# A fused attention, FFN and routed-expert kernel: the router's logits from plain float32 products on four column tiles at once

## The chip, the cores and the metric

The kernel runs on one core of a Trainium2 chip. Its time is the device time of one execution in microseconds (us), as a median over runs. The profile is of one execution.

## The reference

Three stages follow each other on 2304 tokens (4 batches of 576):

```
attn:  8 heads of 64, block-causal softmax attention             -> x [2304, 512]
moe:   h = sigmoid(x @ w_gate) * (x @ w_val)   (d_ff 1536);  x2 = h @ w_out
moe2:  logits = x2 @ w_gate2   (8 experts)
       every token goes to one expert in the order of falling logits, at most 288 tokens an expert
       out[token] = relu(x2 @ w1[e]) @ w2[e]
```

All of it is float32. The assignment of tokens depends on the order of all logits, so these are wanted to float32's full precision.

## The kernel before, in words

TensorE multiplies float32 in two ways here. A *plain* float32 product is one call that appears as two weight loads and two matmuls in the trace. A call on operands stored as F32R (float32r) appears as one weight load and one matmul; for these the kernel splits each operand into a high part (a copy rounded to F32R) and a low part (the difference), and adds the three products high x high, high x low, low x high. The profile's shapes show F32R operands of matmuls as f32 too.

*First half* (`first_half`). For each batch b of 576 tokens, `Ffn.batch` runs 12 tiles f of 128 columns of d_ff. For each tile, two halves hf of 288 tokens; for each half, gate and value: 4 x 3 matmuls of 288 columns into one PSUM bank (L457). ScalarE takes tanh of the gate (L469), VectorE makes h (L470), and SP stores h to memory in the next tile (`store`, L319). While a tile runs, the next tile's weights are split (`split`: ScalarE copies, GpSimd subtracts) and the one after is loaded. `batch` is a generator: each `yield` is a step, and `first_half` uses the steps to interleave other work by count or by cost: attention of the next batch (batches 0 to 2), and every fourth step of batch 3 one advance of `rl` and one of `wo`. `rl` is the chain `relogits(0)`, `relogits(1)`, `f2.first()`; `wo` loads and splits w_out. What is left of `rl` when batch 3 ends is drained there.

*Logits.* As logits are linear in h, the kernel multiplies h by `wog`, the product of w_out and the router's weights, made in batch 1 by `router_weights` (12 tiles of 128 x 8). In batches 2 and 3 (`inline`) h is split while it is made: ScalarE copies it to hh (L472), VectorE subtracts to hl a little later (L474, the list `late`). For every two tiles f, `logits` multiplies hh and hl of both by 128 columns of `wog`, which hold the high and the low part of the weights in columns 0 to 7 and 32 to 39 and zeros elsewhere: 4 matmuls of 288 columns for each half (L410), and VectorE copies or adds the result to `lt` (L414, L416). The last group of batch 3 is in `ffn.close` and is run among the first matmuls of the second FFN, as `CLOSE` counts them. For batches 0 and 1, whose h were made before `wog` existed, `relogits` loads h again, two tiles at a time (L502), splits it (L511 on ScalarE, L512 on VectorE) and multiplies. At the end of each batch `rows` turns `lt` into one row for each token by matmuls with `sel` (L425, L427), which also adds the two partial sums in rows 0 to 7 and 32 to 39.

*Second FFN and router.* `Ffn2.run` multiplies h by w_out, token tile by token tile (L687, 36 products of 512 columns each). `first` loads the first two tiles of h (L647) and splits the first (L660 on ScalarE, L664 on GpSimd), ahead of `run`. The router (`Router.run`) searches the assignment on VectorE with small matmuls and is interleaved with the second FFN's steps by the counts in FILL, FIRST and TAIL; what is left of the second FFN is drained after it. Then the experts follow.

Each engine carries out its instructions in the order in which they were written, and SP issues the DMAs in order too: a load whose buffer isn't free holds up all behind it. All matmuls write to one pool of 8 PSUM banks (`psA`).

Of the kernel before, what the change touches and what calls it, by code (L numbers as in the profile page):

```python
# [8 lines left out]
F32 = mybir.dt.float32  # L9
F32R = mybir.dt.float32r  # L10
BF16 = mybir.dt.bfloat16
I32 = mybir.dt.int32
AF = mybir.ActivationFunctionType
# [3 lines left out]
P = 128  # L17
# [3 lines left out]
def f32(ap):  # L21
    return ap.bitcast(F32)
# [274 lines left out]
class Ffn:  # L297
# [27 lines left out]
    def load(self, b, f, j):  # L325
        k, nc = self.k, self.k.nc
        if b >= k.nb:
            return
        if b == 0:
            x = self.r64.tile([P, 512, 2], I32, name="w64")  # L330
            nc.sync.dma_start(x.rearrange("p (k f) t -> p k (f t)", k=4),
                              (k.w_gate, k.w_val)[j].bitcast(I32)[:, f * 256:(f + 1) * 256]
                              .rearrange("(k p) f -> p k f", p=P))
        else:
            x = self.wf.tile([P, 512], F32, name=f"wf{j}")
            nc.sync.dma_start(x, k.wgv_d[f, j])
        self.raws[b, f, j] = x
# [62 lines left out]
                yield  # L400

    def logits(self, lt, g, hs):
        k, nc = self.k, self.k.nc
        for hf in range(2):
            t = k.psA.tile([P, 512], F32, name="A")
            n = 0
            for f in range(2):
                w = k.wog[:, (2 * g + f) * 64:(2 * g + f) * 64 + P]
                for x in hs[f]:
                    nc.tensor.matmul(t[:, 0:288], w, x[:, hf * 288:(hf + 1) * 288], start=(n == 0), stop=(n == 3))  # L410
                    n += 1
            d = lt[:, hf * 288:(hf + 1) * 288]
            if g == 0:
                nc.vector.tensor_copy(d, t[:, 0:288])  # L414
            else:
                nc.vector.tensor_tensor(d, t[:, 0:288], d, op=OP.add)  # L416
            yield 500

    def rows(self, b, lt):

# [12 lines left out]
    def batch(self, b, inline):  # L433

        k, nc = self.k, self.k.nc
        xt = k.xt[b % 2]
        if inline:
            lt = self.hp.tile([P, 576], F32, name="lt", bufs=1)
        pend, hs, late = None, [], []
        for f in range(12):  # L440
            (gh, gl), (vh, vl) = (self.parts.pop((b, f, j)) for j in range(2))
            todo, at = self.plan(b, f), 0
            h = self.hp.tile([P, 576], F32, name="h")
            if inline:
                hh = self.hp.tile([P, 576], F32R, name="hh", bufs=3)
                hl = self.hp.tile([P, 576], F32R, name="hl", bufs=3)
            for hf in range(2):
                ts = slice(hf * 288, hf * 288 + 288)
                ps = []
                for wh, wl in ((gh, gl), (vh, vl)):  # L450
                    o = k.psF.tile([P, 512], F32, name="A")
                    ps.append(o)
                    for kk in range(4):
                        xh, xl = xt[kk]
                        ks = slice(kk * P, kk * P + P)
                        for n, (w, x) in enumerate(((wh, xh), (wh, xl), (wl, xh))):
                            nc.tensor.matmul(o[:, 0:288], w[:, ks], x[:, ts],  # L457
                                             start=(kk == 0 and n == 0), stop=(kk == 3 and n == 2))
                        if at == 2:
                            self.store()  # L460
                        while todo and todo[0][0] <= at:
                            next(todo.pop(0)[1], None)
                        at += 1
                        if kk == 1 and late:
                            late.pop()()
                        yield 369
                    if len(ps) == 1:
                        sg = self.hp.tile([P, 288], F32, name="sg")
                        nc.scalar.activation(sg, o[:, 0:288], AF.Tanh, scale=0.5)  # L469
                nc.vector.scalar_tensor_tensor(h[:, ts], sg, 1.0, ps[1][:, 0:288], op0=OP.add, op1=OP.mult)  # L470
                if inline:
                    nc.scalar.activation(hh[:, ts], h[:, ts], AF.Copy)  # L472
                    late.append(lambda o=hl[:, ts], x=h[:, ts], y=hh[:, ts]:
                                nc.vector.tensor_tensor(o, x, f32(y), op=OP.subtract))  # L474
            for t in todo:
                next(t[1], None)
            self.stores.append((k.h_d[b][:, f, :], h))
            if inline:
                hs.append((hh, hl))
                if pend:  # L480
                    yield from self.logits(lt, *pend)
                    pend = None
                if len(hs) == 2:
                    pend, hs = (f // 2, hs), []
        self.store()
        for x in late:
            x()
        if inline:
            self.close = (x for g in (self.logits(lt, *pend), self.rows(b, lt)) for x in g)
            if b < k.nb - 1:  # L490
                yield from self.close

    def relogits(self, b):

        k, nc = self.k, self.k.nc
        pool = self.rl
        lt = pool.tile([P, 576], F32, name="lt0", bufs=1)
        flat = lambda x: x.rearrange("p a b -> p (a b)")[:, 0:1152]

        def load(g):  # L500
            h = flat(pool.tile([P, 12, P], F32, name="hraw"))
            nc.sync.dma_start(h.rearrange("p (f t) -> p f t", f=2), k.h_d[b][:, 2 * g:2 * g + 2, :])  # L502
            return h

        def split(h):
            hh = flat(pool.tile([P, 12, P], F32R, name="hh2"))
            hl = flat(pool.tile([P, 12, P], F32R, name="hl2"))
            r = []
            for f in range(2):
                s = slice(576 * f, 576 * f + 576)  # L510
                nc.scalar.activation(hh[:, s], h[:, s], AF.Copy)  # L511
                nc.vector.tensor_tensor(hl[:, s], h[:, s], f32(hh[:, s]), op=OP.subtract)  # L512
                r.append((hh[:, s], hl[:, s]))
            return r

        raw = load(0)
        nxt = None
        for _ in range(4):
            yield 0
        for g in range(7):  # L520
            cur = nxt
            if g < 6:
                nxt = split(raw)
                if g < 5:
                    raw = load(g + 1)
            if cur is not None:
                yield from self.logits(lt, g - 1, cur)
            else:
                yield 0
        yield 0  # L530
        yield from self.rows(b, lt)
# [5 lines left out]
def router_weights(k, ffn):  # L537
# [6 lines left out]
    for ot in ots:  # L544
        nc.gpsimd.memset(ot, 0.0)
    nc.sync.dma_start(mg, k.m_gate.rearrange("(k p) e -> p k e", p=P))
    nc.gpsimd.memset(f32(k.wog), 0.0)
    nc.vector.tensor_scalar(mgs[:, :, 0:8], mg, 0.5, None, op0=OP.mult)
    nc.vector.scalar_tensor_tensor(mgs[:, :, 8:16], mg, 0.5, f32(mgs[:, :, 0:8]), op0=OP.mult, op1=OP.subtract)

# [5 lines left out]
    def product(f, xh, xl):  # L556
        o = k.psA.tile([P, 512], F32, name="A")
        for c in range(4):
            for x in (xh, xl):
                nc.tensor.matmul(o[:, 0:256], mgs[:, c, :], x[:, c, :], start=(c == 0 and x is xh), stop=(c == 3 and x is xl))  # L560
        ot = ots[f // 2 % 2]
        nc.scalar.activation(ot[0:16], o[0:16, 0:256], AF.Copy)
        for _ in range(GAP):
            yield
        o = k.psA.tile([P, 512], F32, name="A")
        for y in range(2):
            nc.tensor.transpose(o[:, P * y:P * y + P], ot[:, P * y:P * y + P], k.ident)
        wt = ffn.cv.tile([P, 2, 16], F32, name="wt16")
        wf = ffn.cv.tile([P, 2, 8], F32, name="wf8")
        nc.vector.tensor_copy(wt, o[:, 0:2 * P].rearrange("p (y e) -> p y e", y=2)[:, :, 0:16])  # L570
        nc.vector.tensor_tensor(wf, wt[:, :, 0:8], wt[:, :, 8:16], op=OP.add)
        d = k.wog[:, f * 64:(f + 2) * 64].rearrange("p (y e) -> p y e", y=2)
        nc.vector.tensor_copy(d[:, :, 0:8], wf)
        nc.vector.tensor_tensor(d[:, :, 32:40], wf, f32(d[:, :, 0:8]), op=OP.subtract)
        yield

    raws = [load(f) for f in range(3)]
# [129 lines left out]

FILL = (((13, 6), (4, 3), (6, 3)), ((8, 3), (4, 3), (6, 3)), 10)
FIRST, TAIL = 8, (15, 35)
CLOSE = (9, 0, 6)  # L710


class Router:
# [480 lines left out]
def tile_fn(ctx, tc, q, kk, v, w_gate, w_val, w_out, m_gate, w1, w2, out, dbg=None):  # L1194
# [13 lines left out]
    k.psF = k.psA  # L1208
    k.ident = const.tile([P, P], F32, name="ident")
    make_identity(nc, k.ident)  # L1210
    k.wog = const.tile([P, 12 * 64 + 64], F32R, name="wogs")
    k.sel = const.tile([P, 8], F32, name="sel")
    nc.gpsimd.memset(k.sel, 0.0)
    for o in (0, 32):
        nc.vector.tensor_copy(k.sel[o:o + 8, :], k.ident[o:o + 8, o:o + 8])
    k.L = const.tile([P, 8, 18], F32, name="logits")
    k.idx = const.tile([P, 24], I32, name="idx")
# [76 lines left out]
```

## Time and profile before

| | |
|---|---|
| median of 3 runs | 1017.5 us (1015.86 to 1019.64) |
| the profiled execution | 1014.82 us |
| its span, first to last instruction | 1013.0 us |
| granted TensorE clock, mean over the span | 0.992 of full speed |
| TensorE busy | 966.7 us (95%), 7387 matmuls |
| VectorE, ScalarE, GpSimd busy | 59%, 45%, 47% |

A busy time counts the shown durations. Matmuls are pipelined: one of 288 columns is shown with 0.29 us, and the next starts 0.13 us after it. So the time that a matmul takes from the stream is read from the start of one to the start of the next.

### The profile page before, as it was taken

The numbers are of one execution on the slowest core, as the hardware profiler recorded it, in microseconds if no ns is written. First come the engines' busy times: TensorE is split into PE (matmuls) and PEld (weight loads), VectorE is DVE, ScalarE is ACT, GpSimd is POOL, SyncE is SP. The second block draws the span as 40 slices with busy tenths as digits, with TensorE's granted clock in tenths as the row PEclk, the third lists the DMA queues.
The fourth block names the chain that finished last, engine by engine and source line by source line (L and its number), as shares of the span: only waits on it lengthen the run. The fifth ranks groups of instructions, "written<-read, shape, count | busy, mean of one in ns | idle before, by whom it ended". The sixth has DMA issues, their size and how long they took to land.

```text
span 1013.0 us, 19715 instructions
## 1 busy us (share of the span) xinstructions
PE 966.7 (95%) x7387; PEld 844.6 (83%) x7387; DVE 601.2 (59%) x1399; ACT 455.9 (45%) x1070; POOL 477.3 (47%) x514
## 2 busy tenths in 40 slices
PE   6899999999999999999999998999998999999996
PEld 4568888879888888888899966666678999999996
DVE  4988898467666445533877467666760444554440
ACT  4775555355555454533554322211121655555551
POOL 2474434334433343453233577776653454455532
PEclk9999999999999999999999999999999999999998
DMA  6755656464554222225576555443433555666640
GB/s 164 188 127 142 211 188 203 132 223 150 186 181 124 89 87 76 67 98 174 172 253 207 167 140 143 128 125 105 123 107 95 184 189 186 212 204 201 196 155 24
DMA packets 191326, 155.18 MB, mean 153 GB/s; under 512 B 70784, under 2 KB 161920, under 8 KB 191232
## 3 DMA queue, kind: packets, MB, share of 16 engines
q1 hardware_dynamic: 187728, 142.92, 46.9%
q0 software_dynamic: 3504, 11.01, 3.1%
q8 instruction: 58, 0.95, 0.4%
q14 instruction: 36, 0.29, 0.1%
HBM read 116.15 MB, written 37.75 MB: 152 GB/s over the span
## 4 chain that ended last, share of the span: by engine, by line
PE 78%; DVE 11%; DMA 3%; issue 3%; SPq 1%; ACT 1%; POOL 1%; POOLq 0%; ACTq 0%; DVEq 0%
PE A L457 27%; PE A L687 10%; PE A L1073 9%; PE A L1118 9%; PE A L211 4%; PE A L116 4%; PE A L163 4%; DVE cmp L852 2%; PE A L836 2%; PE A L122 2%; DVE sub L823 2%; PE A L410 2%; PE A L85 1%; DMA hraw<-h 1%; DVE hl L512 1%
## 5 line engine op out<-in xcount | busy, mean ns | idle before, releaser
L151 POOL TENSOR_SCALAR p<-p,stat 128x128 f32<-128x128 f32 (+2 forms) x144 | 80.2, 569 | 188.6 <-DVE stat L149 132.6
L359 POOL TENSOR_TENSOR w0l<-wf,w0h 128x512 fp32r<-128x512 f32 x48 | 64.9, 1353 | 135.1 <-ACT w0h L357 110.9
L457 PE MATMUL A<-xh,w1h 128*128 128x288 f32 x384 | 121.4, 316 | 1.8 <-ACT ptb L168 1.8
L457 PE MATMUL A<-xh,w0h 128*128 128x288 f32 x384 | 120.5, 314 | 0.0
L457 PE MATMUL A<-xh,w1l 128*128 128x288 f32 x384 | 113.7, 296 | 0.0
L457 PE MATMUL A<-xl,w1h 128*128 128x288 f32 x384 | 113.6, 296 | 0.0
L457 PE MATMUL A<-xh,w0l 128*128 128x288 f32 x384 | 113.2, 295 | 0.0
L457 PE MATMUL A<-xl,w0h 128*128 128x288 f32 x384 | 113.1, 295 | 0.0
L985 POOL TENSOR_TENSOR ewl<-eraw,ewh 128x512 fp32r<-128x512 f32 x56 | 75.0, 1358 | 67.6 <-ACT ewh L981 67.4
L124 DVE TENSOR_REDUCE stat<-A 128x1 f32<-128x128 f32 (+4 forms) x160 | 70.4, 478 | 42.2 <-PE A L122 21.3
L687 PE MATMUL A<-wo_h,hl 128*128 128x512 f32 (+1 forms) x240 | 94.2, 393 | 0.0
L687 PE MATMUL A<-wo_l,hh 128*128 128x512 f32 (+1 forms) x240 | 91.8, 382 | 0.0
L687 PE MATMUL A<-wo_h,hh 128*128 128x512 f32 (+1 forms) x240 | 90.1, 375 | 0.0
L664 POOL TENSOR_TENSOR hl<-hraw,hh 128x512 fp32r<-128x512 f32 x54 | 76.6, 1440 | 28.0 <-ACT hh L660 28.0
L138 ACT ACTIVATE p<-A,stat 128x128 f32<-128x128 f32 (+4 forms) x160 | 81.9, 520 | 16.0 <-DVE stat L124 12.5
L694 ACT ACTIVATE x2r<-A 128x512 f32<-128x512 f32 (+1 forms) x20 | 11.1, 555 | 159.4 <-PE A L687 159.4
L457 PEld LDWEIGHTS A<-xh,w1h 128*128 128x128 f32 x384 | 72.7, 189 | 8.8 <-issue 5.1
L1118 PE MATMUL A<-eh,ewh 128*128 128x288 f32 x256 | 78.0, 305 | 0.0
L1073 PE MATMUL A<-exh,ewh 128*128 128x288 f32 x256 | 77.4, 302 | 0.3 <-ACT exh L1026 0.3
L470 DVE SCALAR_TENSOR_TENSOR h<-sg,A 128x288 f32<-128x288 f32 x96 | 43.1, 449 | 58.3 <-PE A L457 41.3
L457 PEld LDWEIGHTS A<-xh,w0h 128*128 128x128 f32 x384 | 72.3, 188 | 5.8 <-issue 4.2
L1118 PE MATMUL A<-eh,ewl 128*128 128x288 f32 x256 | 75.9, 297 | 0.0
(227 smaller groups left out, 2725.8 us busy)
## 6 DMA issues: line engine op xcount, KB each, us to landing
eraw<-in_moe_w_dram SPq DMA_DIRECT2D x64, 512.0 KB, 4.2
wf<-wgv SPq DMA_DIRECT2D x72, 256.0 KB, 3.9
h<-h SPq DMA_DIRECT2D x48, 288.0 KB, 2.5
hraw<-h SPq DMA_DIRECT2D x16, 768.0 KB, 5.4
hraw<-h SPq DMA_DIRECT2D x12, 576.0 KB, 5.2
w<-in_moe_w_gate_dram SPq DMA_DIRECT2D x12, 512.0 KB, 3.8
w<-in_moe_w_val_dram SPq DMA_DIRECT2D x12, 512.0 KB, 4.1
wgv<-wf SPq DMA_DIRECT2D x24, 256.0 KB, 2.9
```

What stands on the lines that cost most here:

```text
L116: nc.tensor.matmul(s[:, 0:w], qf[r, i * P:(i + 1) * P], kf[r, 0:w], start=True, stop=False)
L124: nc.vector.tensor_reduce(st[:, x:x + 1], s[:, 0:w], axis=AX.X, op=OP.max, negate=True)
L138: nc.scalar.activation(o, s[:, 0:w], AF.Exp, bias=m, scale=1.0, accum_out=st[:, 2 + x:3 + x])
L151: self.k.mark = nc.gpsimd.tensor_scalar(t, t, r[:, x:x + 1], 1.0, op0=OP.mult, op1=OP.mult)
L359: nc.gpsimd.tensor_tensor(l, x, f32(h), op=OP.subtract)
L457: nc.tensor.matmul(o[:, 0:288], w[:, ks], x[:, ts], start=(kk == 0 and n == 0), stop=(kk == 3 and n == 2))
L470: nc.vector.scalar_tensor_tensor(h[:, ts], sg, 1.0, ps[1][:, 0:288], op0=OP.add, op1=OP.mult)
L664: nc.gpsimd.tensor_tensor(l[:, s], x[:, s], f32(h[:, s]), op=OP.subtract)
L687: nc.tensor.matmul(o[:, 0:b - a], x[:, f], w[:, f, a:b], start=(f == 0 and n == 0), stop=(f == 11 and n == 2))
L985: (nc.vector if eng == "v" else nc.gpsimd).tensor_tensor(l[:, s], x[:, s], f32(h[:, s]), op=OP.subtract)
L1073: nc.tensor.matmul(o[:, 0:288], w[:, s], x, start=(d == 0 and n == 0), stop=(d == 3 and n == 2))
L1118: nc.tensor.matmul(o[:, 0:288], w[:, s], x, start=(n == 0), stop=(n == 23))
```

## The change

`logits` now takes h as it is, in plain float32. A group is four tiles f instead of two. For each half it makes four products, one for each f, of 32 columns of weights each, and writes them to the partitions 0 to 31, 32 to 63, 64 to 95 and 96 to 127 of one PSUM bank: each uses its own quarter of the array's columns. Both halves' products are issued in one go, and VectorE's additions come a step later. `rows` adds the four quarters, as `sel` has ones in all four. The splits of h for the logits are gone, in the batches and in `relogits`, which now loads four tiles (two DMAs) for a group, the first two groups at once, into the buffers that held raw and split h. h has 7 buffers, as it is kept until its logits are made; `CLOSE` and the number of steps in `relogits` change.

```diff
     def logits(self, lt, g, hs):
-        for hf in range(2):
-            t = k.psA.tile([P, 512], F32, name="A")
-            n = 0
-            for f in range(2):
-                w = k.wog[:, (2 * g + f) * 64:(2 * g + f) * 64 + P]
-                for x in hs[f]:
-                    nc.tensor.matmul(t[:, 0:288], w, x[:, hf * 288:(hf + 1) * 288], start=(n == 0), stop=(n == 3))
-                    n += 1
+        ts = [k.psA.tile([P, 512], F32, name="A") for _ in range(2)]
+        for hf, t in enumerate(ts):
+            for c, h in enumerate(hs):
+                w = k.wog[:, (4 * g + c) * 32:(4 * g + c) * 32 + 32]
+                nc.tensor.matmul(t[32 * c:32 * c + 32, 0:288], w, h[:, hf * 288:(hf + 1) * 288], start=True, stop=True)
+        yield 1250
+        for hf, t in enumerate(ts):
             d = lt[:, hf * 288:(hf + 1) * 288]
             if g == 0:
                 nc.vector.tensor_copy(d, t[:, 0:288])
             else:
                 nc.vector.tensor_tensor(d, t[:, 0:288], d, op=OP.add)
-            yield 500
+        yield 0
...
     def batch(self, b, inline):
-            h = self.hp.tile([P, 576], F32, name="h")
-            if inline:
-                hh = self.hp.tile([P, 576], F32R, name="hh", bufs=3)
-                hl = self.hp.tile([P, 576], F32R, name="hl", bufs=3)
+            h = self.hp.tile([P, 576], F32, name="h", bufs=7)
...
-                if inline:
-                    nc.scalar.activation(hh[:, ts], h[:, ts], AF.Copy)
-                    late.append(lambda o=hl[:, ts], x=h[:, ts], y=hh[:, ts]:
-                                nc.vector.tensor_tensor(o, x, f32(y), op=OP.subtract))
...
-                hs.append((hh, hl))
+                hs.append(h)
                 if pend:
                     yield from self.logits(lt, *pend)
                     pend = None
-                if len(hs) == 2:
-                    pend, hs = (f // 2, hs), []
+                if len(hs) == 4:
+                    pend, hs = (f // 4, hs), []
...
     def relogits(self, b):
         def load(g):
-            h = flat(pool.tile([P, 12, P], F32, name="hraw"))
-            nc.sync.dma_start(h.rearrange("p (f t) -> p f t", f=2), k.h_d[b][:, 2 * g:2 * g + 2, :])
-            return h
...
             r = []
-            for f in range(2):
-                s = slice(576 * f, 576 * f + 576)
-                nc.scalar.activation(hh[:, s], h[:, s], AF.Copy)
-                nc.vector.tensor_tensor(hl[:, s], h[:, s], f32(hh[:, s]), op=OP.subtract)
-                r.append((hh[:, s], hl[:, s]))
+            for f in range(4 * g, 4 * g + 4, 2):
+                x = pool.tile([P, 12, P], F32, name="hraw") if g % 2 else f32(pool.tile([P, 12, P], F32R, name="hh2"))
+                x = x.rearrange("p a b -> p (a b)")[:, 0:1152]
+                nc.sync.dma_start(x.rearrange("p (f t) -> p f t", f=2), k.h_d[b][:, f:f + 2, :])
+                r += [x[:, 0:576], x[:, 576:1152]]
             return r
-        raw = load(0)
-        nxt = None
-        for _ in range(4):
+        raws = [load(0), load(1)]
+        for _ in range(6):
             yield 0
-        for g in range(7):
-            cur = nxt
-            if g < 6:
-                nxt = split(raw)
-                if g < 5:
-                    raw = load(g + 1)
-            if cur is not None:
-                yield from self.logits(lt, g - 1, cur)
-            else:
+        for g in range(3):
+            yield from self.logits(lt, g, raws.pop(0))
+            if g == 0:
+                raws.append(load(2))
+            for _ in range(3):
                 yield 0
         yield 0
         yield from self.rows(b, lt)
...
-CLOSE = (9, 0, 6)
+CLOSE = (9, 4, 5)
...
-    k.wog = const.tile([P, 12 * 64 + 64], F32R, name="wogs")
+    k.wog = const.tile([P, 12 * 32], F32, name="wogs")
...
-    for o in (0, 32):
+    for o in range(0, P, 32):
         nc.vector.tensor_copy(k.sel[o:o + 8, :], k.ident[o:o + 8, o:o + 8])
```

In `router_weights` the three small VectorE operations that split the weights of two tiles become one that adds them in place.

## Rows read from the trace of the kernel before

**Rows 1.** The page: span, TensorE's busy time, the chain that ended last.
```profile
span 1013.0 us, 19715 instructions
...
PE 966.7 (95%) x7387; PEld 844.6 (83%) x7387; DVE 601.2 (59%) x1399; ACT 455.9 (45%) x1070; POOL 477.3 (47%) x514
...
PE A L457 27%; PE A L687 10%; PE A L1073 9%; PE A L1118 9%; PE A L211 4%; PE A L116 4%; PE A L163 4%; DVE cmp L852 2%; PE A L836 2%; PE A L122 2%; DVE sub L823 2%; PE A L410 2%; PE A L85 1%; DMA hraw<-h 1%; DVE hl L512 1%
```

**Rows 2.** Timeline, TensorE, end of batch 3 (start, time, instruction, count).
```profile
562.17 0.29 PE L457 MATMUL A<-xh,w1l 128*128 128x288 f32 x1
562.30 0.29 PE L410 MATMUL A<-hh,wogs 128*128 128x288 f32 x1
...
563.37 0.29 PE L457 MATMUL A<-xh,w0h 128*128 128x288 f32 x1
...
569.72 0.39 PE L687 MATMUL A<-wo_h,hh 128*128 128x512 f32 x1
569.96 0.39 PE L687 MATMUL A<-wo_l,hh 128*128 128x512 f32 x1
```

**Rows 3.** Windows of line L410 alone: stretch, busy TensorE, weight loads, clock, DMA.
```profile
466.30:570.00 103.70, 24.79 (x136) 19.90 (x136) 1.00 0.61 202
...
370.00:573.00 203.00, 33.95 (x192) 27.84 (x192) 1.00 0.44 143
```

**Rows 4.** Waits, 440 to 580: waiter, releaser, total, times, longest.
```profile
PEld A L410 <- DVE hl L512: 6.1, 9, 1.4
...
PE A L410 <- DVE hl L512: 3.5, 4, 1.2
...
ACT hh L511 <- DMA hraw<-h: 4.6, 3, 3.7
```

**Rows 5.** Timeline, TensorE, end of batch 2 and start of batch 3.
```profile
463.69 0.29 PE L410 MATMUL A<-hl,wogs 128*128 128x288 f32 x1
...
465.15 1.19 PE L425 MATMUL A<-sel,lt 128*128 128x8 f32 x8
...
466.48 0.40 PE L457 MATMUL A<-xh,w0h 128*128 128x288 f32 x1
```

**Rows 6.** Timeline, TensorE: plain float32 products L122 and what follows.
```profile
15.87 1.14 PE L122 MATMUL A<-kf,qd 128*128 128x288 f32 x4
16.84 0.66 PE L163 MATMUL A<-ident,p 128*128 128x128 f32 x4
```

**Rows 7.** Timeline, TensorE, cut at 122.66: the first two of L211.
```profile
122.35 0.49 PE L211 MATMUL A<-ptb,vraw 128*64 128x320 f32 x2
```

**Rows 8.** Timeline, TensorE, 121.9 to 126.2: L211's run of twenty.
```profile
122.12 0.29 PE L457 MATMUL A<-xh,w1l 128*128 128x288 f32 x1
122.35 2.42 PE L211 MATMUL A<-ptb,vraw 128*64 128x320 f32 x20
124.70 1.24 PE L122 MATMUL A<-kf,qd 128*128 128x288 f32 x4
125.56 0.51 PE L457 MATMUL A<-xh,w0h 128*128 128x288 f32 x1
125.91 0.30 PE L457 MATMUL A<-xl,w0h 128*128 128x288 f32 x1
```

**Rows 9.** Line L211: its weight loads, ns least/median/most.
```profile
L211 PEld LDWEIGHTS A<-ptb,vraw x320: 129/137/231, 29.3 to 436.4; 128*64 128x64 f32 x128, 64*64 64x64 f32 x32
```

**Rows 10.** SP's timeline at batch 3's end; lines L647, L660, L664.
```profile
556.70 6.68 SPq L319 DMA_DIRECT2D h<-h  x2
...
DMA to landing us min/median/max: 4.0/5.4/8.2
...
L660 ACT ACTIVATE hh<-hraw x54: 614/621/623, 554.9 to 756.1; 128x512 fp32r<-128x512 f32 x54
...
L664 POOL TENSOR_TENSOR hl<-hraw,hh x54: 1269/1298/1800, 560.3 to 758.7; 128x512 fp32r<-128x512 f32 x54
```

**Rows 11.** Chain of waits, 560 to 800: the router's last work.
```profile
753.71 2.61 DVE ohlo L927 x3
756.69 16.89 PE A L687 x140
```

More of the change, by code (lines that the diff above doesn't have):

```diff
@@ L438, in batch @@
             lt = self.hp.tile([P, 576], F32, name="lt", bufs=1)
-        pend, hs, late = None, [], []
+        pend, hs = None, []
         for f in range(12):
@@ L463, in batch @@
                         at += 1
-                        if kk == 1 and late:
-                            late.pop()()
                         yield 369
@@ L482, in batch @@
                     pend = None
-                if len(hs) == 2:
-                    pend, hs = (f // 2, hs), []
+                if len(hs) == 4:
+                    pend, hs = (f // 4, hs), []
         self.store()
-        for x in late:
-            x()
         if inline:
@@ L497, in relogits @@
         lt = pool.tile([P, 576], F32, name="lt0", bufs=1)
-        flat = lambda x: x.rearrange("p a b -> p (a b)")[:, 0:1152]
         def load(g):
-            h = flat(pool.tile([P, 12, P], F32, name="hraw"))
-            nc.sync.dma_start(h.rearrange("p (f t) -> p f t", f=2), k.h_d[b][:, 2 * g:2 * g + 2, :])
-            return h
-        def split(h):
-            hh = flat(pool.tile([P, 12, P], F32R, name="hh2"))
-            hl = flat(pool.tile([P, 12, P], F32R, name="hl2"))
-            r = []
-            for f in range(2):
-                s = slice(576 * f, 576 * f + 576)
-                nc.scalar.activation(hh[:, s], h[:, s], AF.Copy)
-                nc.vector.tensor_tensor(hl[:, s], h[:, s], f32(hh[:, s]), op=OP.subtract)
-                r.append((hh[:, s], hl[:, s]))
-            return r
-        raw = load(0)
-        nxt = None
-        for _ in range(4):
+            r = []
+            for f in range(4 * g, 4 * g + 4, 2):
[3 more added lines that the diff above has]
+                r += [x[:, 0:576], x[:, 576:1152]]
+            return r
+        raws = [load(0), load(1)]
+        for _ in range(6):
             yield 0
-        for g in range(7):
-            cur = nxt
-            if g < 6:
-                nxt = split(raw)
-                if g < 5:
-                    raw = load(g + 1)
-            if cur is not None:
-                yield from self.logits(lt, g - 1, cur)
-            else:
+        for g in range(3):
[3 more added lines that the diff above has]
+            for _ in range(3):
                 yield 0
@@ L546, in router_weights @@
     nc.sync.dma_start(mg, k.m_gate.rearrange("(k p) e -> p k e", p=P))
-    nc.gpsimd.memset(f32(k.wog), 0.0)
+    nc.gpsimd.memset(k.wog, 0.0)
     nc.vector.tensor_scalar(mgs[:, :, 0:8], mg, 0.5, None, op0=OP.mult)
@@ L568, in product @@
         wt = ffn.cv.tile([P, 2, 16], F32, name="wt16")
-        wf = ffn.cv.tile([P, 2, 8], F32, name="wf8")
         nc.vector.tensor_copy(wt, o[:, 0:2 * P].rearrange("p (y e) -> p y e", y=2)[:, :, 0:16])
[L571 to L574, printed above, removed]
+        d = k.wog[:, f * 32:(f + 2) * 32].rearrange("p (y e) -> p y e", y=2)
+        nc.vector.tensor_tensor(d[:, :, 0:8], wt[:, :, 0:8], wt[:, :, 8:16], op=OP.add)
         yield
```

## The prediction

> **What bounds the kernel now.** I read the page first: TensorE is busy for 95% of the span and makes 78% of the chain that ended last, with the router's logits (L410) 2% of it [rows 1]. Where TensorE is the chain, a change is worth what it takes from or adds to the starts of matmuls, not their shown durations (0.29 us each, overlapping). So I took the timeline of TensorE and read start to start. A group of eight logits products runs from 562.30 to 563.37, and the FFN's last tile from there to 569.72 in 48 products: 1.07 us for a group, 0.133 us a product, 0.132 us for an FFN product [rows 2]. All of them run over 288 columns on the whole array. Then I asked where logits products stand (136 of 192 in batch 3, [rows 3]) and what they wait for: the subtractions L512 of the reloaded h, 9.6 us in 13 waits on two counters that partly overlap [rows 4].
>
> **What the change removes.** Batch 3 begins at 466.48 [rows 5] and ends at 569.72 [rows 2]: 103.2 us. Its FFN takes 12 x 2 x 2 x 12 = 576 products x 0.132 = 76.2. Two `rows` stand in it, each at most the 466.48 - 465.15 = 1.3 of the one behind batch 2 [rows 5]: 2.7. What is left, 24.3 us, are 17 groups (5 of its own, 12 of batches 0 and 1), of which 17 x 1.07 = 18.2 are products and 6.1 stalls. The other seven groups (6 of batch 2, the last of batch 3) are 7.5, plus the wait at the end of batch 2: three starts from 463.69 take 1.46 instead of 0.40, of which I count 0.9 [rows 5]. Together **32.7 us** go. The copies and subtractions on ScalarE and VectorE that go too were worth only those stalls.
>
> **What it adds.** Twelve groups, each of 2 halves x 4 column tiles. A plain float32 product of 288 columns is in the trace: L122 writes two, which appear as four matmuls, from 15.87 to 16.84, so 0.243 us a matmul and two matmuls a product [rows 6]. A new group is thus 16 matmuls: two halves x two passes = 4 sets of four tiles. What four tiles cost together isn't shown. The nearest row is the attention's L211, also plain float32, with two column tiles of 64: two start together [rows 7], and 20 matmuls take from 122.35 to 124.70 = 2.35 us [rows 8]. Their widths sum to (3 x 320 + 192 + 64) x 4 = 4864 columns; at L122's rate (0.243/288 us a column) that is 4.10 us one by one and 2.05 in pairs. So two tiles cost what one does. The ends for a set of four are one pass (0.243) and four (0.97), with two by two (0.486) between. I take 0.243, from the row nearest in kind: a group's products 4 x 0.243 = 0.97 us.
>
> Switching tiling costs as well. Before this run a whole-array product starts at 122.12; 122.12 to 124.70 is 2.58, less 0.13 for that product and 2.05: 0.40. Behind it four L122 matmuls and one L457 last to 125.91, 1.21 instead of 0.97 + 0.13: 0.1 more [rows 8]. The run's last four matmuls are on half the rows, one switch more than here, so 0.40 a group is my value, 0.2 to 0.6 its ends. Twelve groups: 12 x (0.97 + 0.40) = **16.5 us** (14 to 19 by the ends of the switch alone).
>
> By a rule of the Trainium skill ("TensorE: Matmul & The Clock Gate", Part 3, The mechanism) weight loads overlap running matmuls only if their row groups differ; tiles side by side in columns share theirs. The 137 ns loads of L211 [rows 9] would then add ten times 0.137 to that run, 3.4 us instead of 2.35, so the trace contradicts it [rows 8]. By the rule four sets a group would give 12 x 4 x 0.137 = 6.6 us more (an estimate).
>
> **What moves.** Logits of an own batch now wait for no second copy of h: at the end of tile 4 or 8 the last of the four h is a whole tile old, which covers it. Buffers: h goes from 2 to 7; h of tile 0 is read at the end of tile 4 and its buffer wanted at tile 7. Two PSUM banks are held at once until VectorE adds them; it now does 24 such operations instead of 48, and I cost that at nothing.
>
> The recomputed logits of batches 0 and 1 get longer in steps: 23 instead of 19 each (6 + 3 x 5 + 2). They advance once in 4 steps of batch 3, which has 196 steps instead of 202: 49 advances. Two times 23 are 46, so `Ffn2.first` begins its loads at the 47th and its split of token tile 0 falls behind the whole batch; before, it began the split at the 42nd of 50. SP issues that load right behind the store of h of tile 10, whose issue ended at 563.38, 1.2 us after that tile's last matmul started at 562.17 [rows 2, 10]. Counted from the end of batch 3, a tile (6.35 us) later: about -5.2. It lands in 5.4 us [rows 10], at +0.2; ScalarE's first copy takes 0.62, GpSimd's subtraction 1.30 [rows 10], and with 0.1 to 0.2 of handing over the first hl is there at +2.3. The third product of the second FFN wants it at +0.46, as products follow 0.23 to 0.24 apart [rows 2]. So **1.9 us** of stall appear (nothing if the load lands 2 us sooner; 4.7 us at the longest landing of 8.2). The next tiles have 8 us each to catch up.
>
> CLOSE puts 18 products of the second FFN ahead of `rows` instead of 15, which delays the router's start by 3 x 0.23 = 0.7 us against that FFN. After the router's last VectorE work 16.9 us of it are still to run [rows 11], so that is covered; beyond 16.9 us it would not be. The additions in `logits` wait behind the tiled products, and 9 products of 0.23 stand between these and `rows`: 2.1 us for 0.9 us of VectorE.
>
> **The sum.** 32.7 - 16.5 - 1.9 = 14.3 us off the front half, all of it before the second FFN, which with the router and the experts follows unchanged. The profiled execution took 1014.8 (span 1013.0) and would take 1000.5. It lies 2.7 us under the median of the runs, 1017.5, so the median becomes 1003.2; I say 1003.
>
> **The rivals.**
> Two by two: if the moving operands of only two tiles can be fed at once. For it: the trace shows no more than two in columns, and four read twice as much from each partition. Against it: L211's pairs run with no loss at all. A set costs 0.486: 12 x (1.94 + 0.40) = 28.1, so 32.7 - 28.1 - 1.9 = 2.7 off: 1014.8, not told from no change.
> Somewhat less than four: the set costs between 0.243 and 0.486; at 0.307, 12 x 4 x 0.064 = 3.1 are lost: 1006. The Trainium skill (same page, Measured speedup vs the span model) has three column tiles at 2.38 times one, which carried to four is that 0.307, an estimate. L211's pair, 2.0 times one, doesn't show such a loss [rows 8].
> The wait moves to the loads (slower by itself): TensorE now reads the reloaded h straight from its DMA, and each recomputed batch asks for four loads together, ahead of the weights wo. What ScalarE waits for next, the first wo tile, comes up to a landing later, 5.4 us; the PSUM banks that TensorE can fill meanwhile (six or so of 1.6 us each, 12 x 0.132) cover it. If they don't, each of the two batches loses about one landing (5.4) and the second FFN's start the longest (8.2 - 5.4 more): 13.6 lost, 1017 at the worst, 1010 with half of it. For it: ScalarE already waits for such a load [rows 4].
> One after another, the case that is slower: if four narrow tiles don't overlap (the change then doesn't do what it says), a group is 16 x 0.243 + 0.40 = 4.29, twelve 51.5: 20.7 slower, 1038. It decides from a set of about 0.54 us on, (32.7 - 1.9 - 4.8)/48. Against it: rows 7 and 8.
>
> **How the numbers follow.** Chances: four at once 0.61 (by itself 998 to 1007: the switches' ends, the stall's ends and 2 us of the runs' spread), somewhat less 0.09, the loads 0.12, two by two 0.12, one after another 0.06. Under 997 I put little; 1012 takes in all but two by two, one after another and the worst of the loads, some 2 in 10. Half a per cent (5 us) is what this measurement can tell: below 1012.4 is faster: 0.61 + 0.09 + 0.10 of the loads + 0.03 of two by two = 0.83; same 0.10; slower 0.07.
>
> **What would show it.** Right: logits matmuls of 32 columns that start in fours, a group of about 1.4 us start to start, no wait for L512 left, about 16 us in all, and a gap of some 2 us at the first products of the second FFN. Wrong: sets of 0.49 or 0.97 us, or waits of TensorE or ScalarE for hraw and wor in batch 3 that add up to more than a few us.

## The result, and the profile after

The changed kernel takes **1002.26 us** (median of 4 runs, 1000.14 to 1003.31) where the kernel before takes 1018.29 beside it: a ratio of 0.984, 95% interval 0.982 to 0.987, or 16.0 us less (13 to 19). Predicted were 1003 us and 14.3 us less.

In the profiled executions the span fell by 11.5 us only, from 1013.0 to 1001.5: the one before took 1014.82 us, 3.5 under its kernel's median here, the one after 1003.31, 1.0 above. Matmuls of the logits are now counted under L409 (192 matmuls in 96 calls, as before in 192), those of the FFN under L454, of the second FFN under L660; VectorE's compares of the router are L825 (L852 before), GpSimd's subtractions of the second FFN L637 (L664 before). The page, against [rows 1]:

```profile
span 1001.5 us, 19572 instructions
...
PE 955.7 (95%) x7387; PEld 824.4 (82%) x7387; DVE 552.7 (55%) x1293; ACT 425.7 (43%) x998; POOL 475.2 (47%) x514
...
PE A L454 31%; PE A L1046 10%; PE A L1091 9%; PE A L660 9%; PE A L211 5%; PE A L163 4%; PE A L116 4%; DVE cmp L825 3%; PE A L809 2%; DVE sub L796 2%; PE A L122 2%; PE A L409 1%; PE A L85 1%; PE A L996 1%; PE A L1015 1%
```

The wait for L512 and the loads of `hraw` are gone from the lines that the page shows of the chain, and the logits' share is half of what it was. The windows of the logits' line alone, against [rows 3] (stretch, busy TensorE, weight loads, clock, DMA):

```profile
462.50:553.00 90.50, 9.42 (x128) 3.34 (x128) 1.00 0.66 227
...
370.00:557.00 187.00, 14.28 (x192) 5.13 (x192) 1.00 0.45 152
```

One group in the timeline of TensorE, against the eight products in [rows 2], and the first set of that group (the same view, cut at 475.1):

```profile
474.69 0.29 PE L454 MATMUL A<-xl,w0h 128*128 128x288 f32 x1
474.82 0.29 PE L454 MATMUL A<-xh,w0l 128*128 128x288 f32 x1
475.05 1.18 PE L409 MATMUL A<-hh,wogs 128*32 128x288 f32 x16
476.15 0.40 PE L454 MATMUL A<-xh,w1h 128*128 128x288 f32 x1
476.39 0.30 PE L454 MATMUL A<-xl,w1h 128*128 128x288 f32 x1
```

```profile
475.05 0.45 PE L409 MATMUL A<-hh,wogs 128*32 128x288 f32 x4
```

Four matmuls have started by 475.1, as the prediction's sign wanted. From 475.05 to 476.15 are 1.10 us for sixteen matmuls of four tiles f; before, two groups of 1.07 did that. The step into it takes 0.23 instead of 0.13, the one behind it 0.24 instead of 0.13: the steps into and out of the tiled run are 0.1 longer each.

At the start of the second FFN there is the stall that the prediction counted (TensorE after):

```profile
552.97 0.39 PE L660 MATMUL A<-wo_h,hh 128*128 128x512 f32 x1
553.20 0.40 PE L660 MATMUL A<-wo_l,hh 128*128 128x512 f32 x1
554.03 0.50 PE L660 MATMUL A<-wo_h,hl 128*128 128x512 f32 x1 [0.43 <-POOL hl L637]
554.37 0.39 PE L660 MATMUL A<-wo_h,hh 128*128 128x512 f32 x1
```

The fourth product starts 1.17 us behind the second instead of 0.46, so the stall is 0.7 us. The chain of waits gives its parts (start, time, what):

```profile
545.68 0.47 DVE h L465
...
546.16 0.32 SPq L319
...
546.57 5.39 DMA hraw<-h
...
551.98 0.64 ACT hh L633
...
552.69 1.30 POOL hl L637
```

Where the time went, by the starts of TensorE's matmuls in the two profiles:

```
                                       before    after   difference so far
first FFN product of batch 2           340.44   342.37    +1.9
first FFN product of batch 3           466.48   463.72    -2.8
first product of the second FFN        569.72   552.97   -16.8
its 10th product                       572.87   556.96   -15.9
its last product                       773.29   761.30   -12.0
end of the span                       1013.02  1001.47   -11.6
```

So batches 2 and 3 gave 18.7 us. The start of the second FFN took back 0.8, of which 0.7 are the stall and the rest the last group of logits, which lies there. The stretch in which the router and the second FFN share the engines took back 3.9, which the prediction hadn't.

The +1.9 at the start was there before any logits. TensorE's granted clock was lower there (windows 24 to 40, before and after):

```profile
24.00:40.00 16.00, 14.59 (x97) 8.37 (x93) 13.39 (x36) 11.19 (x34) 7.52 (x13) 0.89 0.77 214
```

```profile
24.00:40.00 16.00, 13.97 (x84) 7.89 (x81) 11.90 (x30) 10.55 (x33) 6.05 (x11) 0.79 0.76 212
```

That is 6.8 us at 1.2 instead of 2.4 GHz, where the profile before has 3.4; the lower clock followed an idle time of TensorE of 1.9 us, 1.1 before. It differs between executions (0 to 6.8 us there in the profiles of the other runs), and this one, with 1003.31 us, was the slowest of the four.

Of the 18.7 us, 17.3 are logits. Most of the other 1.4 lies in the attention that batch 2 interleaves. Before, ScalarE's copy of h for the logits (L472) waited for VectorE and stood ahead of a copy of the attention (L168), which TensorE then waited for (ScalarE, then TensorE):

```profile
432.19 0.44 ACT L472 ACTIVATE hh<-h 128x288 fp32r<-128x288 f32 x1 [1.50 <-DVE h L470]
...
433.58 0.58 ACT L168 ACTIVATE ptb<-A 128x512 f32<-128x512 f32 x1
```

```profile
434.21 1.03 PE L211 MATMUL A<-ptb,vraw 128*64 128x320 f32 x6 [1.18 <-ACT ptb L168]
```

After the change L472 is gone, and the list of waits names none of TensorE's matmuls in batch 2. No run takes away L472 alone.

### The profile page after: what moved, and what is told of

It is laid out like the page before. It is cut to its first block, busy times and chain, and to the rows that moved or that the text cites. A ratio compares the mean times of both kernels' runs of the same rounds, so it can differ in the third digit from the quotient of the medians.

```text
span 1001.5 us, 19572 instructions
## 1 busy us (share of the span) xinstructions
PE 955.7 (95%) x7387; PEld 824.4 (82%) x7387; DVE 552.7 (55%) x1293; ACT 425.7 (43%) x998; POOL 475.2 (47%) x514
## 4 chain that ended last, share of the span: by engine, by line
PE 82%; DVE 10%; issue 3%; DMA 2%; POOL 1%; SPq 1%; ACT 1%; DVEq 0%; POOLq 0%; ACTq 0%
PE A L454 31%; PE A L1046 10%; PE A L1091 9%; PE A L660 9%; PE A L211 5%; PE A L163 4%; PE A L116 4%; DVE cmp L825 3%; PE A L809 2%; DVE sub L796 2%; PE A L122 2%; PE A L409 1%; PE A L85 1%; PE A L996 1%; PE A L1015 1%
## 5 line engine op out<-in xcount | busy, mean ns | idle before, releaser
L454 PE MATMUL A<-xh,w1h 128*128 128x288 f32 x384 | 121.7, 317 | 2.0 <-ACT ptb L168 2.0
L454 PE MATMUL A<-xh,w0h 128*128 128x288 f32 x384 | 121.5, 316 | 0.0
L454 PE MATMUL A<-xl,w1h 128*128 128x288 f32 x384 | 113.7, 296 | 0.0
L454 PE MATMUL A<-xh,w1l 128*128 128x288 f32 x384 | 113.7, 296 | 0.0
L454 PE MATMUL A<-xl,w0h 128*128 128x288 f32 x384 | 113.2, 295 | 0.0
L454 PE MATMUL A<-xh,w0l 128*128 128x288 f32 x384 | 113.1, 295 | 0.0
L660 PE MATMUL A<-wo_h,hl 128*128 128x512 f32 (+1 forms) x240 | 94.5, 394 | 0.4 <-POOL hl L637 0.4
L464 ACT ACTIVATE sg<-A 128x288 f32<-128x288 f32 x96 | 39.3, 410 | 127.5 <-PE A L454 123.2
L660 PE MATMUL A<-wo_l,hh 128*128 128x512 f32 (+1 forms) x240 | 91.8, 383 | 0.0
L660 PE MATMUL A<-wo_h,hh 128*128 128x512 f32 (+1 forms) x240 | 90.3, 376 | 0.0
L637 POOL TENSOR_TENSOR hl<-hraw,hh 128x512 fp32r<-128x512 f32 x54 | 76.1, 1437 | 22.6 <-ACT hh L633 21.6
L454 PEld LDWEIGHTS A<-xh,w1h 128*128 128x128 f32 x384 | 72.6, 189 | 10.5 <-issue 6.5
L454 PEld LDWEIGHTS A<-xh,w0h 128*128 128x128 f32 x384 | 72.3, 188 | 9.2 <-issue 5.2
```

Source lines behind the costliest of these rows:

```text
L454: nc.tensor.matmul(o[:, 0:288], w[:, ks], x[:, ts], start=(kk == 0 and n == 0), stop=(kk == 3 and n == 2))
L637: nc.gpsimd.tensor_tensor(l[:, s], x[:, s], f32(h[:, s]), op=OP.subtract)
L660: nc.tensor.matmul(o[:, 0:b - a], x[:, f], w[:, f, a:b], start=(f == 0 and n == 0), stop=(f == 11 and n == 2))
```

## The experiments

**One and two tiles at once.** Do the column tiles run together? In `logits`, with n = 1 or 2 (`rows` then reads 32 n partitions):

```diff
-nc.tensor.matmul(t[32 * c:32 * c + 32, 0:288], w, h[...], start=True, stop=True)
+nc.tensor.matmul(t[32 * (c % n):32 * (c % n) + 32, 0:288], w, h[...], start=(c < n), stop=(c >= 4 - n))
```

> The changed kernel with all four products of a half added up in the first quarter of the columns, one after another (rows reads 32 partitions). Theory (the gain hangs on four tiles running at once): a group is 16 matmuls of 0.243 us instead of 4 sets, 12 x 12 x 0.243 = 35 us more than the changed kernel: 1037, slower than before by 19. Rival (the gain is mostly the removed splits of h and their waits, and tiling adds little): under 1012.

> The changed kernel with two column tiles instead of four: products 2 and 3 are added onto quarters 0 and 1 (rows reads 64 partitions). Theory: 8 sets of 0.243 us a group instead of 4, 12 x 4 x 0.243 = 11.7 us more than the changed kernel: 1014. Rival (two tiles are all that the array feeds at once, or the cost isn't in the sets): the time of the changed kernel, 1002.

Measured: one at a time **1036.11 us** (ratio to the kernel before 1.019, 1.017 to 1.021), two **1014.60** (0.9967, 0.9953 to 0.9981), both within 1 us of the theory. The timelines of TensorE show why. One at a time:

```profile
395.53 4.07 PE L409 MATMUL A<-h,wogs 128*32 128x288 f32 x16
399.52 0.40 PE L455 MATMUL A<-xh,w0h 128*128 128x288 f32 x1
```

Two at a time:

```profile
393.30 2.13 PE L409 MATMUL A<-h,wogs 128*32 128x288 f32 x16
395.36 0.40 PE L455 MATMUL A<-xh,w0h 128*128 128x288 f32 x1
```

The same sixteen matmuls take 3.99, 2.06 and 1.10 us in 16, 8 and 4 sets: (3.99 - 2.06)/8 = 0.24 and (2.06 - 1.10)/4 = 0.24 us a set, however many tiles it holds. Without the tiling the change would have lost 18 us; with pairs it would hardly have been seen.

**What the waits were worth.** The prediction took 7 of its 32.7 us for stalls. First, products that wait for no subtraction, in the kernel before:

```diff
-                for x in hs[f]:
+                for x in (hs[f][0], hs[f][0]):
```

> The kernel before, with the high part of h in the place of its low part in the logits' products (192 products as before; the low part is still made, but no product waits for it; the logits lose the low part of h). Theory: 7 us of the 33 us that the change removes are waits for the subtractions; they go: 1011, and a start-to-start sum of the logits of about 26 us. Rival (the products then wait for the copies and the loads that stand before the subtractions instead): 1015 or more.

Measured 1016.30 us (0.9983, 0.9968 to 0.9997): 1.5 us less, not 7. The logits' start-to-start sum went from 33.0 to 29.6, not to 26, for the products now waited for the copies ahead of the subtractions, as the rival said. Even these 3.4 us didn't all reach the end: other matmuls (L425, L457) now waited up to 4.2 us for VectorE's additions (L416), 0.2 before. Waits in its batch 3 (waiter, releaser, total, times, longest), against [rows 4]:

```profile
PEld A L410 <- ACT hh L511: 2.2, 6, 0.8
...
PE A L410 <- ACT hh L511: 0.6, 1, 0.6
```

Second, the reload a group earlier, all else as before:

```diff
-        raw = load(0)
+        raws = [load(0), load(1)]
...
-                nxt = split(raw)
-                if g < 5:
-                    raw = load(g + 1)
+                nxt = split(raws.pop(0))
+                if g < 4:
+                    raws.append(load(g + 2))
```

> The kernel before, with relogits loading h two groups ahead instead of one (192 products and all splits stay). Theory: the waits of the logits in batch 3 came from reloads that take 5.2 us to land where a group comes every 3.2 us; with two groups' time they go: the logits' start-to-start sum falls from 33.0 to 27 to 28 us, and the time to 1012 to 1014. Rival (the splits' work on VectorE, 0.75 us a copy of h beside all else, is what is late): sum over 31 us, 1016 or more.

Measured 1015.26 us (0.998, 0.9965 to 0.9994), sum 29.5 us: between the two. All products after the first four of batch 3 now run without a gap, but for one set of four, so for them the reload was what came late. The first four of batch 3 still wait for their copies and subtractions, 2.5 us of their 3.0:

```profile
478.26 0.40 PE L410 MATMUL A<-hh,wogs 128*128 128x288 f32 x1
479.13 0.40 PE L410 MATMUL A<-hl,wogs 128*128 128x288 f32 x1 [0.48 <-DVE hl L512]
479.37 0.30 PE L410 MATMUL A<-hh,wogs 128*128 128x288 f32 x1
480.88 0.61 PE L410 MATMUL A<-hl,wogs 128*128 128x288 f32 x1 [1.21 <-DVE hl L512]
```

Both stages, the reload and the split, were thus late by turns, and either remedy alone frees about half of the 7.5 us (33.0 less 192 x 0.133). The change takes both away.

**The router's 3.9 us.** The compares are longer after the change. Their busy time, before and after (windows of that line alone: stretch, VectorE busy):

```profile
573.00:740.00 167.00, 33.08 (x28) 0.99 0.48 135
```

```profile
557.00:727.00 170.00, 38.36 (x28) 0.99 0.48 136
```

One of them, in VectorE's timeline before and after:

```profile
689.88 0.52 DVE L852 TENSOR_SCALAR cmp<-sub,A 128x558 bf16<-128x558 f32 x1 [0.25 <-PE A L846]
```

```profile
674.51 1.62 DVE L825 TENSOR_SCALAR cmp<-sub,A 128x558 bf16<-128x558 f32 x1 [0.26 <-PE A L819]
```

GpSimd's timeline beside it: before, the subtractions start at 691.64, 1.76 us behind the start of that compare; after the change at 674.53, 0.02 behind it (the first one alone):

```profile
691.64 4.29 POOL L664 TENSOR_TENSOR hl<-hraw,hh 128x512 fp32r<-128x512 f32 x3 [2.69 <-ACT hh L660]
```

```profile
674.53 1.29 POOL L637 TENSOR_TENSOR hl<-hraw,hh 128x512 fp32r<-128x512 f32 x1 [0.95 <-ACT hh L633]
```

These subtractions begin when a token tile of the second FFN ends, and the router's place is counted in its products. 18 instead of 15 products ahead of the router put the tile's end three products (0.7 us) earlier in each phase; here a wait of TensorE for the router (0.8) lay between, which makes the shift 1.7. The compare ends 0.3 us behind the end of the subtraction (676.13 and 675.82), as if it had waited for it. By the Trainium skill (SBUF — State Buffer, Who interferes with whom) VectorE's `tensor_scalar` can take a port pair that it shares with GpSimd, and the one that comes second waits for the whole instruction of the other. The rows fit that: 0.52 alone, 1.62 beside a subtraction of 1.3. Which of the two asked first can't be told from 0.02 us. Two kernels put the 15 back, in two ways:

```diff
-CLOSE = (9, 4, 5)
+CLOSE = (9, 0, 6)      # and, in the other kernel, (9, 4, 2)
```

> The changed kernel with CLOSE = (9, 0, 6), so 15 products of the second FFN stand ahead of the last rows instead of 18. Theory (position): with 18, GpSimd's split of the next token tile falls beside the router's compare on VectorE in phases 5 to 7, which took 1.6 us there instead of 0.5; with 15 the router and the second FFN lose that, 2.5 to 4 us, and the time is 998 to 1000. Rival (chance): the router's extra 3.8 us in the profile of the changed kernel differ from run to run; then the time stays at 1002.

> The changed kernel with CLOSE = (9, 4, 2): again 15 products ahead of the last rows, but 4 of them between the logits and their additions, as in the changed kernel. Theory (what counts is how many products of the second FFN precede the router, 15 or 18): 998 to 999.5, with at most 0.5 us of waiting ahead of rows, as VectorE's two additions (0.9 us) have 2 products (0.46 us) less cover. Rival (what counts is the place of the additions): 1001 to 1002, as the changed kernel.

Measured **998.30 us** (0.9805, 0.9783 to 0.9827) and **998.46** (0.9821, 0.9803 to 0.984), as the theory of the count has it, and not that of the place of the additions. The two medians lie 4 us under the changed kernel's, but the intervals overlap its own (0.982 to 0.987). The rows decide: in both the compares are back at what they were before the change, for (9, 0, 6)

```profile
557.00:727.00 170.00, 33.29 (x28) 0.98 0.48 135
```

and for (9, 4, 2)

```profile
557.00:727.00 170.00, 33.18 (x28) 0.98 0.47 131
```

From the 10th to the last product of the second FFN these two profiles take 201.6 and 201.7 us, against 204.3 with 18 products and 200.4 before the change. So 2.7 of the 3.9 us came back. TensorE's granted clock was at 1.2 GHz for 6.8 us of that stretch in both, 3.4 more than in the other two; each fall came within 2 us behind an idle time of TensorE of 1.2 us. That can account for the rest: 3.4 us at half the clock lose 1.7 at the most.

**The stall at the second FFN.** With (9, 0, 6), 4 idle steps less in each relogits:

```diff
-        for _ in range(6):
+        for _ in range(5):
             yield 0
...
-            for _ in range(3):
+            for _ in range(2):
                 yield 0
```

> The kernel with CLOSE = (9, 0, 6) and 4 idle steps less in each relogits (5 instead of 6 ahead, 2 instead of 3 behind each group: 19 steps, as before the change), so the second FFN's first loads and split come 8 advances earlier. Theory: the wait of 0.9 us for GpSimd's first subtraction at the start of the second FFN goes, nothing else waits; 997.4 beside 998.3 without this. Rival (the reloads then land too late for the logits, or the split falls into other work's way): 999 or more, with waits of the logits for hraw.

Measured 999.01 us (0.9812, 0.9791 to 0.9833). The stall is gone, the third product starts 0.24 after the second:

```profile
553.13 0.39 PE L660 MATMUL A<-wo_h,hh 128*128 128x512 f32 x1
553.36 0.40 PE L660 MATMUL A<-wo_l,hh 128*128 128x512 f32 x1
553.60 0.39 PE L660 MATMUL A<-wo_h,hl 128*128 128x512 f32 x1
```

and the logits wait no more than before. In the profiles the first ten products of the second FFN take 3.3 us from first to tenth start, against 4.3 with (9, 0, 6) alone. But that 1.0 us can't be told in the time, whose runs spread over 6.5 us (996.08 to 1002.63). Inconclusive as to time.

The three versions with 15 products (998.3, 998.5 and 999.0 us) can't be told apart. The simplest is the changed kernel with CLOSE = (9, 0, 6): 19.5 us under the kernel before beside it.

## Why the prediction was right, point by point

- *What goes, 32.7 us:* right for the logits. Added up over all 192 products, start to start, they took 33.0 us. That the copies and subtractions "were worth only those stalls" was not: the wait of the attention behind L472 went too, 1.2 us.
- *What comes, 16.5 us:* 15.9. The twelve groups, first matmul to the next instruction's, add up to 13.6 us (1.11 each, 0.3 more at the end of batch 2), and the steps into and out of them are 0.1 longer on each side, 2.3 together. The 0.40 that I put beside 0.97 for switching is thus 0.33 in the group shown: 0.13 inside the run and 0.2 around it.
- *Four at once:* shown by the three tile counts. The rivals of two by two, of somewhat less than four and of one after another fall. L211's pairs were the right row to go by. The rule of the Trainium skill on weight loads ("TensorE: Matmul & The Clock Gate", Part 3, The mechanism) did not hold for four column tiles either: 192 loads of 0.11 us ran beside each other (5.13 us busy in all, above) within sets that follow at 0.24. Nor did the estimate from the same page's 2.38 for three tiles (Measured speedup vs the span model): four gave (3.99 - 1.10)/0.24 = 12 of 16 passes saved, all that can be.
- *The stall of 1.9 us:* there, 0.7 us. The mechanism was right in each part (load 5.39, copy 0.64, subtraction 1.30). The load was issued 6.4 us ahead of the second FFN (546.57 to 552.97), not 5.2, since the `rows` of the second recomputed batch stand in the last tile (about 1.1 us), which I hadn't counted.
- *Loads together, ahead of wo:* covered, as costed. ScalarE waits 11.8 us in 4 times for wor in batch 3, 7.5 the longest, and TensorE waits for none of it: between two FFN products there it never starts later than 0.25 us after the one before. The rival of the loads falls. But the prediction had named a wait of ScalarE of more than a few us as a sign of being wrong; this sign appeared and meant nothing, as only a wait of TensorE would have counted.
- *CLOSE at nothing:* the step that failed. The prediction asked whether 0.7 us of lateness is covered, and it is (16.4 us of the second FFN still followed, from 745.2 to 761.6). It didn't ask what else moves when the router is shifted against the second FFN: GpSimd's subtractions moved onto VectorE's compares, 5.3 us more of these. All of VectorE's work from the 10th to the last product grew by 3.7 us (123.5 to 127.2, as some other instructions got shorter), and the stretch by 3.9.
- *The sum* came out 1.7 us short of the measured 16.0, inside the interval. It was near also because errors cancelled, and that is luck: in the profiles batches 2 and 3 gave 18.7 instead of 16.2 (32.7 - 16.5), the start of the second FFN took 1.1 less than the stall's 1.9, and the router 3.9 more. That makes 14.0; the clock at the start, the end of the span and the spread of the executions lie between this and both the 11.5 of the profiles and the 16.0 of the medians.

## What to carry to other kernels

A whole-array product of which only 16 columns were wanted took as long here as any other (0.133 us). Plain float32 on four column tiles at once cost one tile's start-to-start for all four, 0.24 us a set, and needs no split of its operands, so the copies and the waits behind them go too. Price such a change by starts, from the nearest tiled row, and add some 0.3 us for each run of tiled products (1.3 us for a group, against 4 x 0.243). And when work is interleaved by counts, a change of a count is a change of what runs beside what on the other engines: look at VectorE and GpSimd together at the shifted place, not only at whether the delay is covered.

## What the runs showed of the hardware that was not expected

Four column tiles ran without any loss, which was forecast from pairs alone: 0.24 us a set for one, two and four tiles. A VectorE compare of 128x558 took 0.52 us by itself and 1.62 us when a GpSimd subtraction of 1.3 us started with it.
